# Local attention of one more head pair moved from TensorE to VectorE and GpSimd, and the pace of the later pairs changed

## The chip, the core and the metric

The kernel runs on one core of one Trainium2 chip. The metric is the device time of one execution in microseconds (us), and the time before is the median of three runs. The core's engines run side by side and meet only at semaphores: PE (TensorE, matrix products), DVE (VectorE), ACT (ScalarE), POOL (GpSimd), and the DMA transfers, most of which here are issued from the SP queue. Each engine takes its instructions strictly in the order in which they stand in its own queue.

## The reference

Three stages follow each other. The attention stage has 4 batches of 8 heads, 576 tokens and 64 features per head. Its output is the sum of a pooled attention (over means of 4 neighbouring tokens, repeated 4 times) and a local attention in which a token sees only the 7 tokens at a distance below 4:

```python
factor = 4
q_d = q.reshape(B, H, Sd, factor, D).mean(axis=3)          # k_d, v_d likewise
out_up = np.repeat(sm_attn(q_d, k_d, v_d), factor, axis=2)
mask = np.abs(pos[:, None] - pos[None, :]) < factor
scores = np.where(mask, scale * np.matmul(q, k.transpose(0, 1, 3, 2)), -1e9)
out_local = np.matmul(softmax(scores), v)
x = (out_up + out_local)            # as [2304 tokens, 512]
h = x @ w_in                        # [2304, 2048]
x = (h * sigmoid(1.702 * h)) @ w_out
x = ((x @ w1) * (x @ w2)) @ w3 @ w_out2
```

## The kernel before

**Staging.** The heads are worked in 16 pairs, numbered n = 0 to 15, four to a batch, so pairs 8 to 11 are the third batch and 12 to 15 the fourth. The 2304 tokens of the second stage are cut into five blocks j = 0 to 4 (512, 512, 512, 256 and 512 tokens). Block j is computed while the attention of batch j + 1 is worked in its gaps: block 1 carries pairs 8 to 11, block 2 carries pairs 12 to 15. Block j + 1 begins by reading the attention output `x_d` of its tokens from DRAM (`tok_load`, `tok_split`), and the fourth quarter of the features comes from the last pair of a batch. So block 2 cannot start before pair 11 has been written, nor block 3 before pair 15.

**A block.** For each of 16 slices f of the inner dimension, `h_step` does 12 products of 128x512 into `ps_h` (three passes by `mm3`, since every float32 operand is split into a high and a low part), ACT applies the activation and makes the high part `gh`, DVE the low part `gl` (`split`, L113 and L114). `y_step` for that slice comes two slices later and does 12 more products into `ps_y`. Between these products `pump` puts one piece of the attention at every second place.

**Two ways to do local attention.** The usual way uses TensorE: `s_local` multiplies 64 queries by 72 keys (18 small products per pair, L327), DVE masks and takes the maximum (L330, L331), ACT does the exponentials, `p_piece` transposes nine tiles (L389) and `v_local` does 18 more small products (L416). PSUM tiles of all these steps share the two buffers of pool `pst`: a later step must wait until DVE or ACT has read the tile two steps earlier. For a pair in the table `LOCAL` the work is done without TensorE: `l_load` fetches query, key and value rows (`ql`, `kl`, `vl`), `l_scores` forms a product for each of seven distances o (L457, DVE or for two of them POOL) and sums it (L459, DVE), `l_soft` is the softmax on small tiles (L464 to L471), `l_values` multiplies (L478) and adds (L481), and the result goes to DRAM as `o_d` (L484). `l_out` reads it back transposed (`ost`, L494, L498), adds the pooled part `od` (L501) and writes `x_d` (L504). The pooled attention of every pair stays as it is: `s_pool` (L346, L348), `v_pool` (L404, L407), and for the last batch L371 on DVE.

**Order.** `local_pieces` strings the pairs of `LOCAL` together, 15 pieces a pair after its load. `tick` counts the places between products, from slice 14 of block 0 on, and the number in the table says at every how many places the next piece is put, with a raised priority. The tile framework then schedules the instructions by priority and its own estimates, so the place in the code is not quite the place in an engine's queue. The buffers of pool `stp` (three) hold `ql`, `kl`, `vl`; those of `dp` (two) the products and `ost`.

Of the kernel before, what the change touches and what calls it, by code (L numbers as in the profile page):

```python
# [20 lines left out]
def fused_kernel(ctx, tc, q, k, v, w_in, w_out1, w1, w2, w3, w_out2, out):  # L21
# [20 lines left out]
    PADQ = (NPB - 1) * PB + QB  # L42
    PE_T = 2
    L_F0 = NF - 2
    LOCAL = {12: 3, 13: 3, 14: 4, 15: 4}
    L_PRI = 50
    NM_V = (3,)
    NO = 2 * FAC - 1
# [23 lines left out]
    dram = ctx.enter_context(tc.tile_pool(name="dram", bufs=1, space=DRAM))  # L72
    ldp = ctx.enter_context(tc.tile_pool(name="ldp", bufs=len(LOCAL), space=DRAM))
    psy = ctx.enter_context(tc.tile_pool(name="psy", bufs=1, space=PSUM))
# [157 lines left out]
    def att_load(n, names="qkv", queue=None):  # L232
        b, hp = divmod(n, HP)
        queue = queue or nc.scalar
        for name, src in (("q", q), ("k", k)):
            if name not in names:
                continue
            if b >= PE_T:

                st = att.tile([128, S // 32, 32], F32, tag="s" + name, name="s_" + name)  # L240
                for i in range(4):
                    nc.sync.dma_start(out=st[i * 32:(i + 1) * 32], in_=bass.AP(
                        src.tensor, src.offset + (b * H + 2 * hp + i // 2) * S * D + i % 2 * 32,
                        [[D, 32], [32 * D, S // 32], [1, 32]]))
                at["s" + name, n] = st
                continue
            st = att.tile([UC, 2, FAC, 2, D], F32, tag="s" + name, name="s_" + name)
            for c in range(2):
                queue.dma_start(out=st[:, c], in_=head_ap(
                    src, b, hp, c * UC * FAC, [[FAC * D, UC], [D, FAC], [S * D, 2], [1, D]]))  # L250
            at["s" + name, n] = st
        if "v" not in names:
            return
        st = att.tile([UC, 2, 2, FAC * D], F32, tag="sv", name="s_v")
        queue.dma_start(out=st, in_=head_ap(
            v, b, hp, 0, [[FAC * D, UC], [S * D, 2], [UC * FAC * D, 2], [1, FAC * D]]))
        at["sv", n] = st

    def att_load_v(n):
        b, hp = divmod(n, HP)  # L260
        for t, i0, i1 in ((0, 0, HQ), (1, HQ, NQB)):
            vw = at["vw", n, t] = att.tile([KW, i1 - i0, 2, D], F32, tag=f"vw{t}", name="vw")
            for j0, j1 in ((i0, i0 + 1 - t), (i0 + 1 - t, i1 - t), (i1 - t, i1)):
                tok = min(max(j0 * QB - FAC, 0), S - KW)
                if j1 - j0 == 1:
                    nc.sync.dma_start(
                        out=vw[:, j0 - i0], in_=head_ap(v, b, hp, tok, [[D, KW], [S * D, 2], [1, D]]))
                elif j1 > j0:
                    for h in range(2):
                        nc.sync.dma_start(out=vw[:, j0 - i0:j1 - i0, h], in_=head_ap(  # L270
                            v, b, hp, h * S + tok, [[D, KW], [QB * D, j1 - j0], [1, D]]))
# [63 lines left out]
    def s_pool(n, own_exp):  # L335
        if n % HP == 0 and n > 0:
            att_load(n + 1, "qk")
        near = n not in LOCAL
        if not near:
# [37 lines left out]
    def p_piece(n, i0, i1):  # L377
        if i0 % NPH == 0 and i0 // NPH >= (n in LOCAL):
            at["PT", n, i0 // NPH] = att.tile(
                [KW, min(NPH, NPT - i0), 128], F32, tag=f"PT{i0 // NPH}", name="PT")  # L380
        i0 = i0 if n not in LOCAL else max(i0, NQB)
        ps = pst.tile([KW, i1 - i0, 128], F32, tag="t", name="ps_pt")
        for i in range(i0, i1):
            if i < NQB:
                src = at["el", n][:, i]
            else:
                kc, j = divmod(i - NQB, NPB)
                src = at["ep", n][:, j, kc * UC:(kc + 1) * UC]
            nc.tensor.transpose(ps[:, i - i0], src, ident)  # L389
        nc.scalar.activation(at["PT", n, i0 // NPH][:, i0 % NPH:i0 % NPH + i1 - i0], ps, AF.Copy)  # L390
        first = i0 == (0 if n not in LOCAL else NQB)
        if first:
            v_means(n)
            if n % HP < HP - 1 and n + 2 < B * HP:
                att_load(n + 2, "qk")
# [13 lines left out]
    def v_local(n, i0, i1):  # L409
# [14 lines left out]
        nc.sync.dma_start(out=x_d[:, hp, b * S + i0 * QB:b * S + i1 * QB], in_=xo)  # L424
        if i1 == NQB and n + 1 < B * HP and n + 1 not in LOCAL:
            att_load_v(n + 1)
# [553 lines left out]
```

## Time and profile before

| | us |
|---|---|
| median of 3 runs | 885.12 |
| lowest, highest | 882.38, 891.02 |
| the profiled execution | 888.76 |
| its span, first to last instruction | 886.9 |
| PE busy in the span | 843.2 |
| DVE busy | 589.1 |
| ACT busy | 407.7 |
| POOL busy | 115.2 |

The profile is one execution. Busy shares are means over stages with different limits, so the stage that the change touches (about 240 to 475 us after the span's start) is read by itself.

### The profile page before, as it was taken

The page shows a single profiled execution, that of the slowest core. Times are in us where ns is not written, and L with a number is a line of the kernel's source. Part 1 is how long each engine was busy: PE and PEld are TensorE (multiplying, and loading weights), DVE is VectorE, ACT ScalarE, POOL GpSimd, SP SyncE. Part 2 cuts the span into 40 slices and gives each one's busy share as a digit, 9 for nine tenths or more (in the row PEclk, how much of TensorE's full clock was granted, in tenths as well). Part 3 has the DMA queues.
Part 4 walks back from the last instruction along what each step waited for, and adds up shares of the span by engine and source line. Part 5 has one row for each costly group of instructions (what it writes and reads, how often), then busy time and mean ns, then how long its engine had stood idle before and what let it go on. Part 6 is the DMA issues. An engine that isn't in the chain of part 4 may idle for free.

```text
span 886.9 us, 13686 instructions
## 1 busy us (share of the span) xinstructions
PE 843.2 (95%) x5132; PEld 710.4 (80%) x5132; DVE 589.1 (66%) x1069; ACT 407.7 (46%) x862; POOL 115.2 (13%) x105
## 2 busy tenths in 40 slices
PE   5599989989999999999999999999999999999998
PEld 4477767667677777777789988889999999989996
DVE  5996798779997895847767983253546455545451
ACT  4667677567656666355446663242112211222110
POOL 5323211102342322301200000000000000000000
PEclk9789999999999999999999999999999999999999
DMA  8875784556564344533349988103456364636421
GB/s 226 288 193 154 201 266 144 148 165 175 145 168 98 69 119 101 143 84 74 93 123 355 336 322 334 42 1 111 186 221 253 98 235 177 262 120 234 181 84 71
DMA packets 140598, 150.76 MB, mean 170 GB/s; under 512 B 86898, under 2 KB 121460, under 8 KB 136436
## 3 DMA queue, kind: packets, MB, share of 16 engines
q1 hardware_dynamic: 119424, 141.21, 49.5%
q10 hardware_dynamic: 21108, 8.69, 4.4%
q8 instruction: 40, 0.66, 0.3%
q14 instruction: 26, 0.21, 0.1%
HBM read 117.75 MB, written 32.11 MB: 169 GB/s over the span
## 4 chain that ended last, share of the span: by engine, by line
PE 74%; DVE 12%; DMA 6%; issue 3%; ACT 3%; POOL 1%; SPq 0%; ACTq 0%; DVEq 0%; POOLq 0%
PE ps_ab L119 7%; PE ps_ab L117 7%; PE ps_ab L118 7%; PE ps_h L117 6%; PE ps_y L117 5%; PE ps_h L118 5%; PE ps_y L119 5%; PE ps_h L119 5%; PE ps_y L118 5%; PE ps_o L118 4%; PE ps_o L119 4%; PE ps_o L117 4%; DMA st<-in_moe_w_in_dram 2%; DVE dec L178 2%; DMA st<-in_moe_w_out_dram 2%
## 5 line engine op out<-in xcount | busy, mean ns | idle before, releaser
L117 PE MATMUL ps_h<-x_t,w 128*128 128x512 f32 (+1 forms) x320 | 122.7, 385 | 4.5 <-DVE w L114 4.1
L118 PE MATMUL ps_h<-x_t,w 128*128 128x512 f32 (+1 forms) x320 | 119.7, 374 | 2.7 <-DVE x_t L114 2.7
L117 PE MATMUL ps_y<-gh,w 128*128 128x512 f32 (+1 forms) x320 | 122.1, 382 | 0.0
L118 PE MATMUL ps_y<-gl,w 128*128 128x512 f32 (+1 forms) x320 | 118.8, 371 | 2.1 <-DVE gl L114 2.1
L119 PE MATMUL ps_h<-x_t,w 128*128 128x512 f32 (+1 forms) x320 | 119.1, 372 | 0.0
L119 PE MATMUL ps_y<-gh,w 128*128 128x512 f32 (+1 forms) x320 | 119.0, 372 | 0.0
L119 PE MATMUL ps_ab<-b_t,a_in 128*128 128x384 f32 x336 | 112.5, 335 | 0.0
L117 PE MATMUL ps_ab<-b_t,a_in 128*128 128x384 f32 x336 | 112.5, 335 | 0.0
L118 PE MATMUL ps_ab<-b_t,a_in 128*128 128x384 f32 x336 | 112.4, 334 | 0.0
L114 DVE TENSOR_TENSOR gl<-g_t,gh 128x512 fp32r<-128x512 f32 (+1 forms) x80 | 54.1, 679 | 65.3 <-ACT gh L113 64.8
L618 ACT ACTIVATE g_t<-ps_h 128x512 f32<-128x512 f32 (+1 forms) x80 | 44.3, 555 | 93.6 <-PE ps_h L119 93.3
L113 ACT ACTIVATE abh<-ab 128x384 fp32r<-128x384 f32 x24 | 12.6, 526 | 137.5 <-DVE ab L743 137.5
L117 PEld LDWEIGHTS ps_h<-x_t,w 128*128 128x128 f32 x320 | 60.6, 190 | 18.9 <-DVE w L114 5.9
L118 PEld LDWEIGHTS ps_h<-x_t,w 128*128 128x128 f32 x320 | 61.0, 191 | 13.0 <-DVE x_t L114 4.0
L117 PEld LDWEIGHTS ps_y<-gh,w 128*128 128x128 f32 x320 | 60.3, 189 | 11.8 <-issue 2.4
L118 PEld LDWEIGHTS ps_y<-gl,w 128*128 128x128 f32 x320 | 60.4, 189 | 11.3 <-DVE gl L114 2.7
L119 PEld LDWEIGHTS ps_h<-x_t,w 128*128 128x128 f32 x320 | 60.8, 190 | 10.4 <-issue 0.2
L119 PEld LDWEIGHTS ps_y<-gh,w 128*128 128x128 f32 x320 | 60.4, 189 | 10.4
L117 PEld LDWEIGHTS ps_ab<-b_t,a_in 128*128 128x128 f32 x336 | 63.1, 188 | 0.9
L118 PEld LDWEIGHTS ps_ab<-b_t,a_in 128*128 128x128 f32 x336 | 63.1, 188 | 0.9
L119 PEld LDWEIGHTS ps_ab<-b_t,a_in 128*128 128x128 f32 x336 | 63.1, 188 | 0.0
L178 DVE SCALAR_TENSOR_TENSOR dec<-dec,st 128x512 int32<-128x512 int32 x72 | 57.3, 803 | 2.2 <-ACT dec L165 1.2
(146 smaller groups left out, 1628.7 us busy)
## 6 DMA issues: line engine op xcount, KB each, us to landing
a_in<-a_d SPq DMA_DIRECT2D x24, 1792.0 KB
st<-in_moe_w_dram SPq DMA_DIRECT2D x32, 512.0 KB
a_d<-ap SPq DMA_DIRECT2D x8, 1792.0 KB
st<-in_moe_w_out_dram SPq DMA_DIRECT2D x24, 512.0 KB
st<-in_moe_w_in_dram SPq DMA_DIRECT2D x16, 512.0 KB
yr<-y_d SPq DMA_DIRECT2D x12, 384.0 KB
out_dram<-osb SPq DMA_DIRECT2D x17, 256.0 KB
s_v<-in_v_dram ACTq DMA_DIRECT2D x15, 288.0 KB
```

The costliest lines, as they stand in the source:

```text
L113: nc.scalar.activation(hi, raw, AF.Copy)
L114: lo_eng.tensor_tensor(lo, raw, f32(hi), op=ALU.subtract)
L117: nc.tensor.matmul(ps, ll, rh, start=start, stop=False, skip_group_check=more)
L118: nc.tensor.matmul(ps, lh, rl, start=False, stop=False, skip_group_check=more)
L119: nc.tensor.matmul(ps, lh, rh, start=False, stop=stop, skip_group_check=more)
L178: nc.vector.scalar_tensor_tensor(t, t, 3, st[:, :, 0], op0=ALU.logical_shift_left, op1=ALU.bitwise_or)
L618: nc.scalar.activation(g[:, :n], ps[:, :n], AF.Gelu_apprx_sigmoid)
```

## The change

The table gets an entry for pair 11, the last of the third batch, whose local attention is then done by the second way, at every second place; pairs 14 and 15 go from every fourth place to every third. With pair 11 first in the string, the total is 215 places instead of 214.

```diff
-    LOCAL = {12: 3, 13: 3, 14: 4, 15: 4}
+    LOCAL = {11: 2, 12: 3, 13: 3, 14: 3, 15: 3}
```

PE loses 18 L327, 9 L389 and 18 L416. DVE gains 5 L457, 7 L459, 5 L478, 6 L481, seven small softmax steps, two L498 and two L501, and loses two each of L330, L331, L305 and L420. POOL gains two L457 and two L478 and loses one L369. ACT loses nine exponentials (L307) and two copies (L390) and gains one small exponential.

The first place is DVE's queue in block 1, where `s_local` of pair 10 is reached (`el` is its masked score tile, `prod` the products of a pair of the table). Before:

```order
L481 TENSOR_TENSOR ql_3145<-ql_3145,prod_3616 128x576
L114 TENSOR_TENSOR gl_3442<-g_t_3439,gh_3441 128x512
L330 TENSOR_TENSOR el_3472<-ps_s_3477,band_97 128x360
L331 TENSOR_REDUCE mx_3474<-el_3472 128x5
L305 TENSOR_SCALAR nb_3476<-mx_3474 128x5
L330 TENSOR_TENSOR el_3472<-ps_s_3506,band_97 128x288
L279 STREAM_TRANSPOSE qT_3633<-s_q_3406 128x576
L331 TENSOR_REDUCE mx_3474<-el_3472 128x4
L279 STREAM_TRANSPOSE kT_3658<-s_k_3411 128x576
L305 TENSOR_SCALAR nb_3476<-mx_3474 128x4
L348 TENSOR_REDUCE mx_3474<-ps_sp_3534 128x3
L457 TENSOR_TENSOR prod_3649<-ql_3638,kl_3640 128x576
```

The same place in DVE's queue now:

```order
L481 TENSOR_TENSOR ql_3025<-ql_3025,prod_3448 128x576
L114 TENSOR_TENSOR gl_3459<-g_t_3456,gh_3458 128x512
L457 TENSOR_TENSOR prod_3490<-ql_3480,kl_3482 128x576
L457 TENSOR_TENSOR prod_3543<-ql_3480,kl_3482 128x576
L459 TENSOR_REDUCE s_3489<-prod_3490 128x9
L459 TENSOR_REDUCE s_3489<-prod_3543 128x9
L330 TENSOR_TENSOR el_3496<-ps_s_3501,band_97 128x360
L457 TENSOR_TENSOR prod_3577<-ql_3480,kl_3482 128x576
L331 TENSOR_REDUCE mx_3498<-el_3496 128x5
L459 TENSOR_REDUCE s_3489<-prod_3577 128x9
L305 TENSOR_SCALAR nb_3500<-mx_3498 128x5
L330 TENSOR_TENSOR el_3496<-ps_s_3527,band_97 128x288
```

The first two products and sums of the next pair of the table (pair 13 now, pair 14 before) moved ahead of both L330.

The second place is SP's queue where one pair of the table ends and the next is loaded, first in block 1. Before, the result is written and then the next pair's three tiles are fetched:

```order
L242 DMA s_k_3023<-in_k_dram 32x18x32 x4
L484 DMA o_d_3128<-ql_2662 128x576
L432 DMA ql_3145<-in_q_dram 128x576
L439 DMA kl_3147<-in_k_dram 128x960
L439 DMA vl_3149<-in_v_dram 128x960
```

The same place in SP's queue now:

```order
L432 DMA ql_3025<-in_q_dram 128x576
L242 DMA s_q_3042<-in_q_dram 32x18x32
L637 DMA y_d_93<-ys_2875 128x512
L637 DMA y_d_93<-ys_2881 128x512
L242 DMA s_q_3042<-in_q_dram 32x18x32
L242 DMA s_k_3047<-in_k_dram 32x18x32 x2
L439 DMA kl_3027<-in_k_dram 128x960
L484 DMA o_d_2999<-ql_2662 128x576
```

The fetch of `kl` moved ahead of the write of `o_d`, and that of `ql` further ahead still; the next such place, before pair 13, has `kl` ahead of `o_d` too.

The third place is DVE's queue at the end of block 2, where `l_out` of pair 15 stands (`x_t` is the split input of block 3, `gl` of the last slices of block 2). Before:

```order
L114 TENSOR_TENSOR gl_4849<-g_t_4846,gh_4848 128x512
L498 STREAM_TRANSPOSE xo_4820<-ost_4815 128x320
L501 TENSOR_TENSOR xo_4820<-xo_4820,od_4807 128x320
L178 SCALAR_TENSOR_TENSOR dec_5042<-dec_5042,st_5017 128x512
L498 STREAM_TRANSPOSE xo_4836<-ost_4831 128x256
L501 TENSOR_TENSOR xo_4836<-xo_4836,od_4807 128x256
L114 TENSOR_TENSOR gl_4880<-g_t_4877,gh_4879 128x512
```

The same place in DVE's queue now:

```order
L114 TENSOR_TENSOR gl_4902<-g_t_4899,gh_4901 128x512
L114 TENSOR_TENSOR x_t_4952<-xr_4948,x_t_4952 128x256
L114 TENSOR_TENSOR x_t_4957<-xr_4950,x_t_4957 128x256
L498 STREAM_TRANSPOSE xo_4811<-ost_4806 128x320
L501 TENSOR_TENSOR xo_4811<-xo_4811,od_4798 128x320
L178 SCALAR_TENSOR_TENSOR dec_5033<-dec_5033,st_5008 128x512
L114 TENSOR_TENSOR gl_4933<-g_t_4930,gh_4932 128x512
L498 STREAM_TRANSPOSE xo_4827<-ost_4822 128x256
L501 TENSOR_TENSOR xo_4827<-xo_4827,od_4798 128x256
```

The four steps of `l_out` of pair 15 moved behind the first two `x_t` and to both sides of the last `gl` of the block; before, they stood ahead of the last two `gl` and of every `x_t` of block 3.

## Rows read from the trace of the kernel before

**Rows 1.** The page, part 1: busy us, share of the span, instructions

```profile
PE 843.2 (95%) x5132; PEld 710.4 (80%) x5132; DVE 589.1 (66%) x1069; ACT 407.7 (46%) x862; POOL 115.2 (13%) x105
```

**Rows 2.** Busy us by stretch: length, PE, PEld, DVE, ACT, POOL, clock, DMA, GB/s

```profile
300.00:380.00 80.00, 78.53 (x536) 60.69 (x536) 62.57 (x102) 45.41 (x104) 27.89 (x20) 1.00 0.49 125
...
412.00:460.00 48.00, 48.00 (x247) 37.87 (x246) 31.78 (x60) 21.36 (x43) 5.82 (x5) 1.00 0.44 112
```

**Rows 3.** Timeline, PE, block 1: s_local of pair 11 (start, length)

```profile
339.82 0.40 PE L119 MATMUL ps_h<-x_t,w 128*128 128x512 f32 x1
340.15 0.85 PE L327 MATMUL ps_s<-kT,qT 64*64 64x72 f32 x20
...
341.26 0.39 PE L118 MATMUL ps_y<-gl,w 128*128 128x512 f32 x1
...
342.19 0.40 PE L119 MATMUL ps_y<-gh,w 128*128 128x512 f32 x1
...
343.50 0.40 PE L118 MATMUL ps_y<-gl,w 128*128 128x512 f32 x1
```

**Rows 4.** Timeline, PE: products around a transposing piece, pair 11, then a later pair

```profile
356.38 0.39 PE L119 MATMUL ps_h<-x_t,w 128*128 128x512 f32 x1
...
357.28 0.40 PE L118 MATMUL ps_y<-gl,w 128*128 128x512 f32 x1
...
409.88 0.39 PE L119 MATMUL ps_h<-x_t,w 128*128 128x512 f32 x1
...
410.67 0.39 PE L118 MATMUL ps_y<-gl,w 128*128 128x512 f32 x1
```

**Rows 5.** Timeline, PE: the products around v_local of pair 11

```profile
367.19 0.39 PE L119 MATMUL ps_y<-gh,w 128*128 128x512 f32 x1
...
369.05 0.40 PE L118 MATMUL ps_y<-gl,w 128*128 128x512 f32 x1
```

**Rows 6.** Groups of DVE instructions, 240 to 460 us, shapes apart: busy, mean ns

```profile
L459 DVE TENSOR_REDUCE s<-prod 128x9 f32<-128x576 f32 x28 | 20.3, 744 | 6.2 <-POOL prod L457 6.2
L457 DVE TENSOR_TENSOR prod<-ql,kl 128x576 f32<-128x576 f32 x20 | 18.2, 918 | 4.7 <-DMA kl<-in_k_dram 3.9 <-issue 0.7
```

**Rows 7.** Timeline, PE: its two longest waits from 240 to 480 us

```profile
291.96 0.95 PE L346 MATMUL ps_sp<-kd,qd 64*64 64x144 f32 x12 [1.54 <-DVE el L330]
...
379.86 0.50 PE L118 MATMUL ps_h<-x_t,w 128*128 128x512 f32 x1 [1.30 <-DVE x_t L114]
```

**Rows 8.** Timeline, DVE and SP queue: one pair of the table ends, the next begins

```profile
312.35 1.42 DVE L478 TENSOR_TENSOR prod<-vl,s 128x576 f32<-128x576 f32 x2
...
315.75 0.53 DVE L330 TENSOR_TENSOR el<-ps_s,band 128x360 f32<-128x360 f32 x1
...
321.11 0.76 DVE L457 TENSOR_TENSOR prod<-ql,kl 128x576 f32<-128x576 f32 x1 [0.87 <-DMA kl<-in_k_dram]
...
316.17 0.41 SPq L439 DMA_DIRECT2D kl<-in_k_dram  x1
```

**Rows 9.** Timeline, PE: s_pool of pair 10

```profile
318.63 0.95 PE L346 MATMUL ps_sp<-kd,qd 64*64 64x144 f32 x12
```

**Rows 10.** Timeline, DVE: the same change of pairs, one pair earlier

```profile
278.65 0.76 DVE L457 TENSOR_TENSOR prod<-ql,kl 128x576 f32<-128x576 f32 x1 [3.00 <-DMA kl<-in_k_dram]
```

**Rows 11.** Timeline, DVE: s_pool of pair 15, its maximum and its scaling

```profile
435.54 0.59 DVE L348 TENSOR_REDUCE mx<-ps_sp 128x3 f32<-128x432 f32 x1
...
438.56 0.61 DVE L371 TENSOR_TENSOR ep<-ep,sm 128x432 f32<-128x432 f32 x1
```

**Rows 12.** Timeline, SP queue and DVE: pair 11 written, last input of block 2

```profile
371.26 0.35 SPq L424 DMA_DIRECT2D x_d<-xo  x1
...
379.13 0.68 DVE L114 TENSOR_TENSOR x_t<-xr,x_t 128x512 fp32r<-128x512 f32 x1
```

**Rows 13.** Timeline, DVE and PE: last gl of block 2, first product of block 3

```profile
468.22 0.69 DVE L114 TENSOR_TENSOR gl<-g_t,gh 128x512 fp32r<-128x512 f32 x1
...
474.24 0.28 PE L117 MATMUL ps_h<-x_t,w 128*128 128x256 f32 x1
```

## The prediction

> **What bounds the kernel now.** I read the page first: PE is busy for 843.2 of 886.9 us and DVE for 589.1 [rows 1], so PE sets the pace over the span, and what the change is worth is what it does to PE's stream. Then I cut the span by stages. In 300 to 380 us, the main part of block 1, PE is busy for 78.53 of 80 us and DVE for 62.57 [rows 2]; PE has no slack there and DVE has 17.4 us, but in pieces between waits. Third, PE's timeline from 240 to 480 us, looking for brackets, that is, idle time and who ended it. Two of them are over 1 us [rows 7]: 1.54 us before the `s_pool` of pair 9, whose PSUM buffer DVE had not yet read, and 1.30 us at the start of block 2, where the last quarter of its input arrives late. The rest of this stage runs almost without a gap on PE, so each us of PE work removed here is a us of span, as long as the DVE work that replaces it is never waited for.
>
> **What the change removes from PE.** Products of 128x512 start every 0.23 us when nothing lies between them: the four steps from 341.26 to 342.19 take 0.93 [rows 3]. The cost of an inserted piece is the distance of the products around it less that pitch.
> - `s_local` of pair 11: 339.82 to 341.26 is 1.44 us for two steps, so 0.98 extra, and 342.19 to 343.50 is 1.31, so 0.85 extra [rows 3]. Together 1.83.
> - transposes: a piece of four tiles costs 357.28 - 356.38 = 0.90, less 0.46, so 0.44; a piece of a table pair with three tiles costs 410.67 - 409.88 = 0.79, so 0.33 [rows 4]. Pair 11 has three pieces of four and one of three now and two of three afterwards: 1.65 - 0.66 = 0.99.
> - `v_local`: 369.05 - 367.19 = 1.86, less 0.46, so 1.40 [rows 5].
>
> The sum is 4.2 us, and all of it lies on the path. The nine exponentials and two copies that leave ACT are worth nothing by themselves beyond that, since ACT is busy for 45.41 of these 80 us [rows 2] and ends neither of the two waits [rows 7].
>
> **What it adds to DVE, and where.** 23 of the added instructions pass over 576 elements, at 0.744 (L459) to 0.918 us (L457, with its slow ones beside POOL) [rows 6]: 17 to 21 us, and some 4 us of small ones, less about 3 us of L330, L331, L305 and L420. That is 18 to 22 us. DVE's order says where: to the end of block 1 there are three pairs' values before and after, and only two L457, three L459 and pair 11's `l_out` more, so block 1 takes about 3 us net and block 2 the other 16 or so. Added up, DVE can hold it. What counts is the order in the queue, at four places.
>
> *First change of pairs.* Pair 12's `kl` is now fetched ahead of the write of pair 11's result. Before, DVE sat idle for 3.00 us for that fetch and began the next scores at 278.65 [rows 10]; those scores stand ahead of the `el` step whose lateness cost PE 1.54 us [rows 7]. If they start 2 to 3 us earlier, that wait shrinks to little. I take 1.3 us of gain, between a gain of 1.5 and, should the two transposes that now stand among the scores eat it up, a loss of 1.
>
> *Second change of pairs, the new wait.* This is the step I trust least and the largest cost. At pair 10's `s_local`, two L457 and two L459 of pair 13 now stand ahead of the L330 that frees the PSUM buffer for `s_pool`. L457 must wait for `kl`. By the rows of the same place: the last L478, which frees the buffer for `kl`, ends at 313.77; before, `kl` was issued at 316.17 and used at 321.11, 4.94 us later, with `ql` and the result's write in flight beside it [rows 8]. Issued at 313.8, it would be usable at 318.7. Four instructions take 2.8 and L330 0.53 (it ran at 315.75 before, at no one's expense [rows 8]), so the buffer is free at 322.1. PE wanted it at 318.5, since L346 began at 318.63 [rows 9]. PE then waits 3.6 us, with everything behind L346 in its queue. Bounds: if the fetch takes half as long, being issued first now, 1.1; if `kl` in the end goes out no sooner than before, 4.94 from 316.17 and then 3.3, that is 324.4, so 5.9; and none if DVE runs further ahead of PE here than it did. I take 3.6.
>
> The Trainium skill, page "DMA: Bandwidth & Descriptors", section "Anatomy of one DMA — SWDGE (gpsimd) path", fits a transfer as about 2.0 us fixed plus its bytes at 436 GB/s, for transfers that GpSimd issues. An estimate by it is 3.1 us for these 480 KB, the wait would be 1.8 us and the whole sum 1.8 us lower; the row above, with its companions in flight, is longer and no run of this kernel shows the fetch alone.
>
> *Start of block 2.* Pair 11's last step on PE is now `v_pool`, 24 products (5.5 us) earlier in PE's queue than `v_local` was with respect to block 2, which covers DVE's two L498 and two L501 and the write. The last input step came at 379.13, 7.9 us after the write was issued at 371.26 [rows 12]; moved ahead by that much, it stands clear of the need. So the wait of 1.30 us [rows 7] goes: a gain of 1.3, or none if `l_out` is itself held up by pair 14's scores, among which its steps are placed.
>
> *Pair 15's `s_pool`.* Before, DVE took 435.54 to 439.17 from L348 to the end of L371, with 6 instructions between [rows 11]. Now 21 stand between: seven long ones more (0.744 to 0.918 [rows 6], 5.8 us), four `l_out` steps (estimate 0.45 each, from the 0.53 of L330 [rows 8]) and four small ones (0.2 each, an estimate), so 8.4 us longer, 12.0 in all, counted from the end of L346, 0.95 after its start: 13.0. PE has in the meantime L346 (0.95), `v_pool` (0.7, an estimate by the same row) and 45 products of 0.23, so 12.0. It waits 1.0 us; bounds 0 and 3, since waits for POOL's products can come on top.
>
> *Start of block 3.* Pair 15's `l_out` now stands behind the first two `x_t` and around the last `gl`, which cannot run before the last `h_step`; it began at 468.22, and block 3 at 474.24 [rows 13]. The second L501 then ends at about 469.8. Block 3 needs its fourth quarter after nine products of half width, at 475.3: 5.5 us for the write, the read and two splits, which took 8.6 at the start of block 2 with twice the width and other transfers beside it [rows 12]. I take a wait of 1.0, between 0 and 3.1. Before, there was none.
>
> **Sum.** -4.2 - 1.3 - 1.3 + 3.6 + 1.0 + 1.0 = -1.2 us. The profiled execution took 888.76 us, 1.9 more than its span and 3.6 more than the median, 885.12. So 887.6 for an execution like it, and 883.9 as a median.
>
> **Rivals.**
> - *The cover holds.* `kl` lands before DVE gets to it, and none of the new waits appears. For it: DVE has 17.4 us idle in 300 to 380 [rows 2], and the fetch is issued earlier. Against it: four instructions in front of L330 are a matter of the order and not of the load. Then -4.2 - 1.3 - 1.3 = -6.8, so 878.3.
> - *Pair 15 is late and block 3 waits (slower).* Its scores now start behind pair 14's L348, so that about 12 us of DVE work moved into the last 50 us of block 2, and then `o_d` must be written, read back, added, written as `x_d` and read again. Without the last term the sum is -2.2, so from a wait of 2.2 us on at block 3 the change loses. For it: the chain of 8.6 us [rows 12] against the 5.5 us left, and `l_out` placed as late as it can be. Against it: the stretch needs only about 44 of 48 us of DVE (31.78 before [rows 2] and the 12), and the transfer is half as wide. With a wait of 6 us the time is 885.1 - 2.2 + 6 = 888.9; to lose 1% it would have to be 11.
> - *The change does not do what it says.* PE's queue has lost exactly the three groups of pair 11, so this has almost no chance.
>
> **How the numbers follow.** The forecast, gains and new waits that nearly cancel (881 to 887), gets 0.60; the cover that holds, 0.20; the late pair 15, 0.17; anything else 0.03. The range of 8 in 10 reaches to both rivals: 877.5 to 890. A change under 1%, 8.9 us, can hardly be told from none. Faster by over that needs every gain and something unseen: 0.05. Slower by over that needs the late pair at its worst together with the 5.9 us: 0.06. Within it 0.89.
>
> **What would show it.** In the profile of the changed kernel: PE's busy time down by some 4 us; an idle bracket of 2 to 5 us before L346 ended by DVE `el` at pair 10, about 315 us in, with L457 waiting for `kl` just ahead of it; no bracket of over 0.5 us at that place for pair 9 nor at the first `x_t` of block 2; brackets of about 1 us before pair 15's L389 and in the first slice of block 3. I am wrong if PE is idle elsewhere in blocks 1 and 2, above all before a `ps_y` product that waits for `gl`, for then DVE's total, and not its order, has become the bound.

## The result, and the profile after

The changed kernel took 894.43 us (median of 9 runs, 889.16 to 899.68) beside 885.12 us before: ratio 1.0107, 95% interval 1.0083 to 1.0132. It is slower by 1.1%. The forecast was 883.9 with a range up to 890.0, so it was wrong, in its sign and in its range.

The page's part 1, in the profiled execution (894.43 us, span 892.6), answers to [rows 1]:

```profile
PE 842.0 (94%) x5051; PEld 708.7 (79%) x5051; DVE 609.7 (68%) x1095; ACT 407.1 (46%) x847; POOL 119.0 (13%) x108
```

The work moved as forecast: 81 PE records fewer (each of the 36 small products of L327 and L416 is recorded twice, each of the nine transposes once), and 20.6 us more on DVE, where 18 to 22 were expected. But PE is busy for almost as long as before, where 4.2 us less were expected, and it waits more. The windows of the changed kernel (length, PE, PEld, DVE, ACT, POOL, clock, DMA, GB/s) show where; the first and the last answer to [rows 2], and the two in between cover the longest new waits:

```profile
300.00:380.00 80.00, 74.93 (x450) 57.91 (x449) 66.76 (x105) 39.01 (x80) 24.65 (x19) 0.98 0.44 109
345.00:353.00 8.00, 5.21 (x46) 3.77 (x46) 6.46 (x14) 3.94 (x9) 1.56 (x2) 0.79 0.72 222
380.00:391.00 11.00, 8.39 (x37) 5.66 (x36) 10.74 (x14) 4.30 (x8) 2.98 (x2) 0.84 0.38 84
412.00:460.00 48.00, 46.34 (x241) 36.58 (x240) 36.78 (x64) 22.03 (x41) 8.96 (x7) 1.00 0.29 66
```

In those two short windows the kernel before has PE busy for all 8.00 and 11.00 us, at a granted clock of 1.00. Now PE stands, and the mean granted clock falls to 0.79 and 0.84 besides. PE's timeline from 240 to 480 us gives the brackets (idle time and who ended it) of over 0.5 us (answers to [rows 7]):

```profile
278.75 0.63 PE L389 MATMUL ps_pt<-ident,el 128*72 128x128 f32 x4 [1.35 <-POOL el L369]
...
319.31 0.71 PE L404 MATMUL ps_vp<-PT,vd 72*64 72x144 f32 x8 [0.51 <-DVE el L330]
...
328.42 1.27 PE L416 MATMUL ps_v<-PT,vw 72*64 72x64 f32 x36 [1.37 <-ACT ep L307]
...
348.46 0.80 PE L416 MATMUL ps_v<-PT,vw 72*64 72x64 f32 x20 [2.79 <-ACT ep L307]
...
386.60 0.52 PE L118 MATMUL ps_y<-gl,w 128*128 128x512 f32 x1 [2.36 <-DVE gl L114]
...
455.08 0.82 PE L389 MATMUL ps_pt<-ident,ep 128*72 128x128 f32 x6 [1.66 <-DVE ep L371]
```

Both waits of before are gone (1.54 at `ps_sp`, 1.30 at `x_t`), and six others are there, 10.0 us in all. The last was in the forecast as it came, and the second is a small remnant of another forecast wait (see the part on the second change of pairs below); the other four, 7.9 us, were not.

The longest one, followed back. PE has `v_local` of pair 10 in its queue and needs a PSUM buffer; the buffer holds `ps_sp` of pair 11 until ACT has taken its exponentials, and these wait for the maximum (L348) and its scaling (L305) on DVE, which stand behind pair 13's values:

```profile
342.00 1.41 DVE L478 TENSOR_TENSOR prod<-vl,s 128x576 f32<-128x576 f32 x2
343.33 1.28 DVE L481 TENSOR_TENSOR ql<-ql,prod 128x576 f32<-128x576 f32 x1
344.54 0.59 DVE L348 TENSOR_REDUCE mx<-ps_sp 128x3 f32<-128x432 f32 x1
345.06 0.68 DVE L114 TENSOR_TENSOR gl<-g_t,gh 128x512 fp32r<-128x512 f32 x1
345.66 0.15 DVE L305 TENSOR_SCALAR nb<-mx 128x3 f32<-128x3 f32 x1
...
345.91 1.28 ACT L307 ACT_TABLE_LOAD   x1 [4.76 <-DVE nb L305]
...
347.94 0.38 ACT L307 ACTIVATE ep<-ps_sp,nb 128x144 f32<-128x144 f32 x1
...
351.40 0.63 PE L118 MATMUL ps_h<-x_t,w 128*128 128x512 f32 x1
351.83 0.63 PE L119 MATMUL ps_h<-x_t,w 128*128 128x512 f32 x1
```

The last two rows show the second price: after that wait products start every 0.43 us instead of 0.23, the lower of PE's two levels. ACT adds to the first: of the 2.5 us from its start at 345.91 until the buffer is read, 1.28 are the load of its table for the exponential.

The wait of 1.37 us at 328.42, for the exponentials of `s_pool` of pair 10, has another chain. Its scaling ended on DVE at 322.73, but ACT came to those exponentials only at 325.36. ACT had stood until 318.97 for the scaling of pair 10's local scores, which had pair 13's scores ahead of it on DVE, and then loaded its table three times, as a step of the activation (L618) stood between the local exponentials and the pooled ones:

```profile
322.03 0.70 DVE L305 TENSOR_SCALAR nb<-mx 128x3 f32<-128x3 f32 x1
...
318.97 1.28 ACT L307 ACT_TABLE_LOAD   x1 [8.14 <-DVE nb L305]
...
323.44 1.28 ACT L618 ACT_TABLE_LOAD   x1
...
325.36 1.28 ACT L307 ACT_TABLE_LOAD   x1
```

The wait at 386.60 is the one that the prediction named as the sign of its own failure. The `gl` of the first slice of block 2 stands behind pair 14's values:

```profile
383.57 0.75 DVE L478 TENSOR_TENSOR prod<-vl,s 128x576 f32<-128x576 f32 x1
384.35 1.59 DVE L481 TENSOR_TENSOR ql<-ql,prod 128x576 f32<-128x576 f32 x1
385.86 0.68 DVE L114 TENSOR_TENSOR gl<-g_t,gh 128x512 fp32r<-128x512 f32 x1
```

The big products of the second stage are the same 1920 in every kernel here (128x512, those of block 3 128x256), so their starts serve as milestones. The table gives the time from one of them to the next in us, worked out from the traces (block 1 starts at number 384, block 2 at 768, block 3 at 1152):

| kernel | 384 to 480 | to 576 | to 660 | to 768 | to 830 | to 1010 | to 1152 | sum |
|---|---|---|---|---|---|---|---|---|
| before | 27.4 | 32.3 | 26.1 | 33.4 | 17.2 | 48.9 | 33.8 | 219.2 |
| changed | 27.7 | 30.5 | 28.3 | 33.5 | 20.9 | 48.7 | 35.6 | 225.1 |
| pace alone | 26.7 | 31.4 | 26.1 | 33.4 | 21.2 | 49.2 | 33.5 | 221.5 |
| pair alone | 28.4 | 37.3 | 27.4 | 30.9 | 15.7 | 48.6 | 35.7 | 224.1 |
| without pair 11's local attention | 32.8 | 30.5 | 27.7 | 29.7 | 20.2 | 48.7 | 36.1 | 225.7 |
| pause | 29.5 | 30.5 | 28.2 | 34.7 | 15.2 | 48.6 | 36.1 | 222.9 |
| no maximum | 28.5 | 30.5 | 27.3 | 29.2 | 19.3 | 48.7 | 33.9 | 217.4 |
| pause, no maximum | 29.8 | 30.6 | 27.3 | 29.2 | 16.6 | 48.7 | 34.4 | 216.5 |
| before, no maximum | 26.7 | 31.6 | 26.1 | 33.4 | 15.6 | 49.2 | 33.5 | 216.2 |
| those two, norm first | 28.1 | 30.5 | 27.3 | 29.2 | 16.6 | 48.7 | 34.4 | 214.7 |

A sum is one execution, and single ones differ by some us. That of before was 3.6 us above its median, and part of this lies in the table: the pace alone, and the pace with the pause (further down), have the same order as before in the queues of PE, DVE, ACT and GpSimd from number 384 to 576, and take 58.1 and 58.5 us for it instead of 59.7. The wait of 1.54 us at `ps_sp` is 0.61 and 0.63 there:

```profile
285.97 0.95 PE L346 MATMUL ps_sp<-kd,qd 64*64 64x144 f32 x12 [0.61 <-DVE el L330]
...
293.33 0.95 PE L347 MATMUL ps_sp<-kd,qd 64*64 64x144 f32 x12 [0.63 <-DVE el L331]
```

So the loss of 5.9 us in the table is less than the 9.3 between the medians, and no trace shows all of the difference. Verdicts below go by the runs; the table says only where.

### The profile page after: what moved, and what is told of

It reads as the page before. It is cut to its first block, busy times and chain, and to the rows that moved or that the text cites. A ratio compares the mean times of both kernels' runs of the same rounds, so it can differ in the third digit from the quotient of the medians.

```text
span 892.6 us, 13551 instructions
## 1 busy us (share of the span) xinstructions
PE 842.0 (94%) x5051; PEld 708.7 (79%) x5051; DVE 609.7 (68%) x1095; ACT 407.1 (46%) x847; POOL 119.0 (13%) x108
## 4 chain that ended last, share of the span: by engine, by line
PE 70%; DVE 15%; DMA 6%; issue 4%; ACT 3%; POOL 1%; ACTq 0%; SPq 0%; DVEq 0%; POOLq 0%
PE ps_ab L117 7%; PE ps_ab L119 7%; PE ps_ab L118 7%; PE ps_h L117 5%; PE ps_y L117 5%; PE ps_y L119 5%; PE ps_y L118 5%; PE ps_h L118 5%; PE ps_h L119 5%; PE ps_o L118 4%; PE ps_o L119 4%; PE ps_o L117 4%; DVE dec L178 3%; DMA st<-in_moe_w_out_dram 2%; DVE ql L481 2%
## 5 line engine op out<-in xcount | busy, mean ns | idle before, releaser
L114 DVE TENSOR_TENSOR gl<-g_t,gh 128x512 fp32r<-128x512 f32 (+1 forms) x80 | 51.7, 648 | 58.8 <-ACT gh L113 58.5
L618 ACT ACTIVATE g_t<-ps_h 128x512 f32<-128x512 f32 (+1 forms) x80 | 44.1, 553 | 85.6 <-PE ps_h L119 81.0
```

What stands on the lines that cost most here:

```text
L114: lo_eng.tensor_tensor(lo, raw, f32(hi), op=ALU.subtract)
L618: nc.scalar.activation(g[:, :n], ps[:, :n], AF.Gelu_apprx_sigmoid)
```

## The experiments

Theory A: pair 11's DVE work comes ahead of short steps that PE needs soon. Rival B: the pace of pairs 14 and 15 does it. Rival C: DVE's total has become the bound. Ratios are to runs of the kernel before on the same chip, with the 95% interval.

### The change taken apart

```diff
-    LOCAL = {11: 2, 12: 3, 13: 3, 14: 3, 15: 3}
+    LOCAL = {12: 3, 13: 3, 14: 3, 15: 3}           # pace alone
+    LOCAL = {11: 1, 12: 2, 13: 3, 14: 4, 15: 4}    # pair alone
```

> Only the new pace: pairs 14 and 15 at every third place, pair 11 stays on PE as before. Theory A (pair 11's added DVE work, put into DVE's in-order queue in blocks 1 and early 2, stands ahead of short steps that PE needs soon): the waits of ps_v for ACT's exponentials and of ps_y for gl go, the start of block 2 keeps its 1.30 us wait, and the time is 885 (883 to 888). Rival B (it is the faster pace of pairs 14 and 15 that crowds DVE in block 2): the waits stay in good part and the time is 890 to 895. Rival C (DVE's total work is the bound): the work is that of the kernel before, so 885, but then the waits should also be spread over many places in the changed kernel.

> Only the pair: pair 11's local attention on DVE and GpSimd, pairs 14 and 15 keep every fourth place; to fit, pair 11 goes at every place and pair 12 at every second. Theory A (pair 11's work ahead of short steps): PE still waits for several us in blocks 1 and 2, 889 to 895. Rival B (the pace of 14 and 15): the waits go, PE's saving of 4.2 us shows, 881 to 885. Rival C (DVE's total): as the changed kernel, 894.

The pace alone: 888.70 us, 1.0058 (1.0028 to 1.0089). The pair alone: 891.76, 1.0103 (1.0076 to 1.0129). So neither A nor B alone: each part loses. In the table the pace loses at one place, the start of block 2 (21.2 against 17.2). The pair alone passes that place in 15.7, and loses in block 1, 37.3 against 32.3 before number 576, where its trace has two waits of 2.90 and 3.27 us for GpSimd's `el`.

```diff
+                if n == 11:                        # local_pieces; x_d of pair 11 then gets od alone
+                    yield lambda: None, 1 + 15 * every
+                    continue
```

> The changed kernel without pair 11's local attention: neither PE nor DVE and GpSimd compute it (its places stay empty, and its x_d holds the pooled part alone). All theories have PE's saving here; what remains is the saving without its price on DVE. Saving as predicted: 885.1 - 4.2 - 1.3 - 1.3 = 878 to 881, and no wait of over 1 us for DVE or ACT in blocks 1 and 2. If the loss is from the pace of pairs 14 and 15 (rival B), waits remain in block 2 and the time is 886 to 890.

> Pair 11's local attention is done twice: on PE as before the change, and its DVE and GpSimd steps run too, in the places of the changed kernel, with a result that nobody uses. So PE has none of the saving and DVE has all of the added work. If the cost of the added DVE work is separate from the saving: 894.4 + 4.2 = 898.6 (896 to 902). If PE's own work covers DVE's (the longer PE takes, the later it needs DVE): close to the changed kernel, 892 to 895.

Without any local attention of pair 11: 891.94, 1.0092 (1.0062 to 1.0122), a miss for all three theories. From 660 to 768 PE takes 29.7 instead of 33.4, so the saving is there; but the waits for `gl` (3.08 us) and for pair 15's L371 (1.89) stay though DVE has none of pair 11's work, and an input wait of 3.07 us comes at the start of block 1. What is late in block 2 is late though DVE has no more to do than before (busy for 591.0 us in all, 589.1 before); what has changed is where the pairs behind pair 11 stand. This speaks against C. With the work done both ways: 895.40, 1.0138 (1.0111 to 1.0165), 0.3% over the changed kernel, where 0.5% was the saving by itself; the intervals overlap, so this decides nothing.

### Steps put ahead by priority

```diff
+            with tc.high_priority(100):      # scores first: all steps of s_local, s_pool from pair 8 on
+        with tc.high_priority(100 if j > 0 else 0):   # split first: gelu, gh, gl
-    L_PRI = 50
+    L_PRI = 0                                # no priority
```

> The changed kernel, with the scores of the pairs of the later batches (L330, L348, the maxima and L305) put ahead of the local pieces in DVE's queue. Theory A (order in DVE's queue): the two waits of ps_v for the exponentials (4.2 us, and the low clock behind them) go or shrink under 1 us, so 5 to 6 us come back: 888 to 890; the waits for gl at 386 us and for pair 15's L371 stay. Rival C (DVE's total, or what the tables of places do to the whole stretch): the waits come back elsewhere, 893 to 896.

> The changed kernel, with the gelu and the split into gh and gl of all slices but the first of a batch put ahead of the local pieces. Theory A: the wait of 2.4 us for gl in block 2's first slice goes, with the low clock behind it, 3.5 us in all: 890 to 892; the two waits of ps_v stay. Rival C: no change, 893 to 896.

> Both orders together. Theory A: about 9 us of the loss come back and PE's saving shows, 884 to 887. Rival C: 892 to 896. A second rival: local pieces pushed back make the later pairs late (pair 15's L371 and l_out), then a longer wait at 455 us or a new one at the start of block 3, 888 to 892.

> The changed kernel with the local pieces given no priority at all (L_PRI 0 in place of 50), so that each stands in DVE's queue where the program writes it. Theory A: if their early place is what makes PE wait, the waits of ps_v and of gl shrink: 886 to 890; if the written places already stand ahead of the short steps, no change, 893 to 896. Rival C: 893 to 896.

Scores first 894.03 (1.0109, 1.0089 to 1.0130), split first 894.21 (1.0109, 1.0081 to 1.0138), both 909.48 (1.0277, 1.0246 to 1.0307), no priority 898.38 (1.0159, 1.0136 to 1.0182). None gained. These edits were too broad to decide between A and C: a priority on a piece moves its products too, and PE's queue differs from the changed kernel's in some 20 (no priority) to 50 places (both). With both first, PE's timeline has the scores scattered singly among the products:

```profile
277.01 0.34 PE L327 MATMUL ps_s<-kT,qT 64*64 64x72 f32 x2
277.28 0.50 PE L117 MATMUL ps_y<-gh,w 128*128 128x512 f32 x1
277.71 0.34 PE L327 MATMUL ps_s<-kT,qT 64*64 64x72 f32 x2
```

From 277.28 to the next product at 277.97 is 0.69 us instead of 0.23, and eighteen products in a row take 0.69 to 0.82; four waits of 1.2 to 2.3 us for the input, the activation and GpSimd's `el` stand in front (7.0 us). So PE needs 44.7 us from 384 to 480. Narrower edits came next.

### One wait at a time

The first edit keeps the local pieces off the start of block 2 and catches up afterwards; PE's queue keeps its order but for pair 15's last steps. The second takes DVE out of the chain in front of `ps_v`: the pooled scores of pairs 8 to 15 go to the exponential without their maximum.

```diff
-                if wait[0] <= 0:
+                place[0] += 1
+                if wait[0] <= 0 and not 136 <= place[0] < 152:
                     fn, wait[0] = next(local, (None, 1))
+                    wait[0] = wait[0] if place[0] < 152 else 2
```

```diff
-        nc.vector.tensor_reduce(mx, ps, op=ALU.max, axis=X)
-        if own_exp:
+        flat = own_exp and n >= 2 * HP
+        if not flat:
+            nc.vector.tensor_reduce(mx, ps, op=ALU.max, axis=X)
+        if flat:
+            for i in range(NPB):
+                nc.scalar.activation(ep[:, i], ps[:, i], AF.Exp, scale=PSCALE, accum_out=sm[:, i:i + 1])
+        elif own_exp:
```

> The changed kernel, with no local piece put from place 136 to 152 (the last slice of block 1 and the first of block 2), and one at every second place after that. PE's queue stays as it is but for pair 15's transposes. Theory D (PE waits where DVE's queue is full over some 10 us, whatever its total): the wait of 2.4 us for gl at the start of block 2 and the low clock behind it go (3.7 us), so 889 to 891, and 888 if pair 15's wait of 1.7 us goes too, since its pieces end 10 places earlier; the two waits of ps_v in block 1 stay. Rival C (DVE's total): the waits come back in block 2, where DVE now has as much to do in less time, 893 to 897.

> The changed kernel, where the pooled scores of pairs 8 to 15 go to the exponential without the maximum taken off first, so that ACT no longer waits for L348 and L305 on DVE. Order theory: the two waits of ps_v for ACT's exponentials (4.2 us, and about 1 us at the low clock behind them) go, 888 to 890; the wait for gl at the start of block 2 stays. If ps_v then waits for something else in the same place, 893 to 895.

> Both: the pause at the start of block 2 and the pooled scores without their maximum. If the two losses are separate, both gains add: 894.4 - 5 - 5 = 884 (882 to 887), at or under the kernel before, and PE's saving of 4 us shows in block 1. If DVE's total is the bound, 891 to 895.

> The kernel before, with the pooled scores of pairs 8 to 15 without their maximum: a control for the other two. Its trace shows only 0.5 us of wait for ACT's exponentials, so the edit should give it at most that and some DVE time: 883 to 886. If it gains as much as the changed kernel does (4 us or more), then it was not pair 11's move that made these steps late.

The pause: 891.12, 1.0080 (1.0056 to 1.0104). No maximum: 888.75, 1.0056 (1.0034 to 1.0079). Both: 883.82, 0.9987 (0.9969 to 1.0005). The kernel before without the maximum: 884.54, 1.0007 (0.9986 to 1.0029). Each edit takes away its own wait: with the pause nothing over 0.4 us is left at the start of block 2 (15.2 against 20.9), while the two of `ps_v` stay at 1.37 and 2.78; without the maximum these are 0.94 and none, while `gl` stays at 2.35. Together they give back the whole loss, 1.2% of the time, and the control shows that the second is worth nothing to the kernel before: it was the move of pair 11 that made these steps late. Alone they give 0.3%, which the intervals do not set apart from none, and 0.5%. That both give more than the sum is within the intervals of the four ratios (0.2% each way), and in the table the gains are 2.2, 7.7 and 8.6 us, so not more than the sum.

The second edit does more than it was meant to. The two `ps_v` stand four and five products earlier in PE's queue, with less cover than in the changed kernel. But `s_pool` of pair 15 moves as well, from number 1007 to 999 (972 before), and the wait of 1.66 us for its L371 is gone (33.9 against 35.6 in the last column). And ACT loads its table 25 times from number 384 to 1152, as in the kernel before, where the changed kernel has 29. So not all that this edit gives back need come from the maximum, and these runs don't separate the three. Nor was the pause given to the kernel before, whose trace has a wait of 1.30 us at that place. What PE still waits for with both, from 260 to 480 us:

```profile
277.98 0.63 PE L395 MATMUL ps_pt<-ident,el 128*72 128x128 f32 x4 [2.04 <-POOL el L375]
...
326.24 1.27 PE L422 MATMUL ps_v<-PT,vw 72*64 72x64 f32 x36 [0.94 <-ACT ep L354]
...
378.16 0.50 PE L119 MATMUL ps_y<-gl,w 128*128 128x512 f32 x1 [0.59 <-DVE gl L115]
```

### Where the saving stays

With both edits PE's 4.2 us are visible (29.2 against 33.4 to number 768), and yet the kernel only equals the one before. The wait at 277.98 is at the first change of pairs, where the prediction booked a gain: pair 12's scores now start earlier, and stand ahead of the two small steps (L365, L366) after which GpSimd scales pair 8's `el`. In the changed kernel:

```profile
275.12 1.02 DVE L365 TENSOR_SCALAR sm<-sm 128x12 f32<-128x12 f32 x1
...
276.81 0.22 DVE L366 RECIPROCAL sm<-sm 128x12 f32<-128x12 f32 x1
...
274.68 1.43 POOL L457 TENSOR_TENSOR prod<-ql,kl 128x576 f32<-128x576 f32 x1 [12.08 <-DVE s L459]
277.18 1.52 POOL L369 TENSOR_TENSOR el<-el,sm 128x648 f32<-128x648 f32 x1 [1.07 <-ACT g_t L618]
```

```diff
+        with tc.high_priority(60 if n // HP == 2 else 0):    # norm first: L365, L366 and the scalings
```

> As the kernel with both edits (pause, pooled scores without maximum), and the normalisation of pairs 8 to 11 (L365, L366 of the kernels before) put ahead of the local pieces; in DVE's queue only pair 8's two steps move, ahead of one L457 and two L459, and PE's queue keeps its order but for two products. Order theory: PE's wait of 2.04 us at 278 us for GpSimd's el of pair 8 goes, because the sums reach GpSimd about 2 us earlier: 883.8 - 2 = 882 (881 to 883). If GpSimd's own queue is what is late there (its L457 ahead of the scaling), no change, 883 to 885.

> As the kernel with both edits, and the local scores of pairs 8 to 15 without their maximum too: 22 instructions less on DVE, some 8 us over blocks 1 and 2. If DVE's load in those blocks still costs PE about 5 us (the saving of 4 us is in, the kernel stands at 883.8), part of it comes back: 879 to 882. If only single places in the order matter, 882 to 886, as they fall.

> The kernel before with pooled and local scores of pairs 8 to 15 without maximum: the control for the run with 22 instructions less. 40 instructions less on DVE than before. Since its PE waits for DVE only at two places (1.5 and 1.3 us), it gains at most 3 us: 882 to 885. If it gains as much as the changed kernel, pair 11's move is worth nothing once DVE is eased.

Norm first: 882.18, 0.9976 (0.9951 to 1.0001); the wait shrinks from 2.04 to 0.50, and 384 to 480 from 29.8 to 28.1. No maximum in the local scores either (22 DVE instructions less): 885.77, 1.0025 (0.9995 to 1.0055), no gain over 883.82, and its control 883.25, 0.9988 (0.9955 to 1.0020). So less work on DVE buys nothing that can be measured. Two small steps moved ahead of three long ones buy 1.7 us in that stretch of the traces; by the runs it is 0.1%, with intervals that overlap, so the gain in time is not shown. The run without pair 11's work, the pace alone (DVE busy for 590.1 us, and a loss) and the run with 22 instructions less all speak against C.

### The pace by itself

> The faster pace of pairs 14 and 15 alone (pair 11 on PE as before), with no local piece from place 136 to 152, around the start of block 2. The pace alone took 888.7, with 3.9 us lost at the start of block 2. Theory D: that loss goes, 884 to 886. If the pace costs wherever it is, 888 to 890.

The pace with the pause: 889.49, 1.0067 (1.0038 to 1.0097), as without it. So the local pieces at the start of block 2 are not what the pace alone pays for. The timeline of the pace alone, without the pause, PE and DVE:

```profile
370.38 0.49 PE L117 MATMUL ps_h<-x_t,w 128*128 128x512 f32 x1
373.57 0.79 PE L118 MATMUL ps_h<-x_t,w 128*128 128x512 f32 x1 [2.71 <-DVE x_t L114]
374.17 0.63 PE L119 MATMUL ps_h<-x_t,w 128*128 128x512 f32 x1
374.59 0.63 PE L117 MATMUL ps_h<-x_t,w 128*128 128x512 f32 x1
...
371.51 1.41 DVE L459 TENSOR_REDUCE s<-prod 128x9 f32<-128x576 f32 x2 [1.31 <-POOL prod L457]
372.84 0.68 DVE L114 TENSOR_TENSOR x_t<-xr,x_t 128x512 fp32r<-128x512 f32 x1
```

The last input step starts 4.5 us after the block's first product (368.34), in the kernel before after 4.8 (379.13 [rows 12] less 374.32). But before, six products of the block's second slice stand in PE's queue ahead of those that need it (the wait is at number 784, here at 778): 1.4 us less cover. And behind the longer wait 13 products run at 0.43 instead of 0.23, which is 2.6 us. The two make the 4.0 that the table shows.

```diff
+            with tc.high_priority(100 if kk == KD - 1 and j in (2,) else 0):   # (1, 2) in the second kernel
                 tok_split(j, kk)
```

> The faster pace of pairs 14 and 15 alone, with the split of the last quarter of block 2's input put ahead of the local pieces; with that edit PE's queue has products of the second slice ahead of those that need this quarter (in the pace alone they stand behind). The pace alone lost 3.9 us at the start of block 2, in a wait of 2.71 us for that quarter and 13 products at the low clock behind it. If that wait is the whole price of the pace: 888.7 - 4 = 884.7 (883 to 886). If the pace costs DVE's place elsewhere in block 2: 887 to 889.

> The kernel with three edits (pause, pooled scores without maximum, normalisation of pairs 8 to 11 first), with the last quarter of the input of blocks 1 and 2 split first as well. Its PE still waits 0.70 us for that quarter at the start of block 1 and 0.62 us for gl in block 2: 881 to 882.2; if moving these steps makes others late, 882.5 to 885.

With that input split first the pace alone takes 886.65, 1.0034 (1.0015 to 1.0053): the wait is 1.69 and no product runs slowly behind it. If this is the gain that the ratios show (0.6% to 0.3%, with intervals that overlap), it explains somewhat under half of the pace's loss; the rest stays open. The changed kernel with the three edits and this one takes 880.72, 0.9976 (0.9954 to 0.9997), 0.2% under the kernel before and 1.3% under the changed one.

## Why the prediction was wrong, point by point

- **What PE saves, 4.2 us.** Right: 33.4 to 29.2 where nothing else is late. In the changed kernel itself the waits of `ps_v` hide it.
- **First change of pairs, a gain of 1.3.** Right in its direction, too large: the wait of 1.54 is gone, and 480 to 576 takes 1.8 less than in the trace of before. But with the order of before that wait was 0.6 us in two other executions, so about half of the gain belonged to the one that was profiled. And the same earlier scores made pair 8's `el` late, 1.35 us, which was not looked for; moved back, those two steps gave 1.7 us in the trace.
- **Second change of pairs, a new wait of 3.6.** Mis-sized: at L346 it did not come. Three steps of the order were as said (the fetch, two L457 and two L459, L330), but all of it ran earlier:

```profile
309.27 0.35 SPq L439 DMA_DIRECT2D kl<-in_k_dram  x1
...
312.80 1.43 DVE L457 TENSOR_TENSOR prod<-ql,kl 128x576 f32<-128x576 f32 x2 [1.53 <-DMA kl<-in_k_dram]
...
315.47 0.52 DVE L330 TENSOR_TENSOR el<-ps_s,band 128x360 f32<-128x360 f32 x1
...
316.25 0.95 PE L346 MATMUL ps_sp<-kd,qd 64*64 64x144 f32 x12
```

  `kl` went out at 309.27, not at the 313.8 that was taken from the trace of before [rows 8], and was used 3.5 us later, not 4.9. What was left of the wait came at the next step that needs a buffer of the pair, `v_pool`: 0.51 us for the second L330 of pair 10, which still had pair 13's scores ahead of it. The estimate of 3.1 us from the Trainium skill, page "DMA: Bandwidth & Descriptors", section "Anatomy of one DMA — SWDGE (gpsimd) path", lies nearer to the trace than mine, although it is for transfers that GpSimd issues.
- **Start of block 2, a gain of 1.3.** The input is in time (a wait of 0.22 instead of 1.30, [rows 7]). But PE then stands for 2.36 us before `ps_y`, and the stretch lengthens by 3.7. The prediction had said that such a wait would mean that DVE's total is the bound. The sign was right and its reading wrong: the pause took it away with the same DVE instructions (1095).
- **Pair 15, 1.0.** Right in kind, 1.66 in size. DVE took 12.5 us from L348 (442.40) to the end of L371 (454.93), where 12.0 were added up [rows 11]:

```profile
442.40 0.61 DVE L348 TENSOR_REDUCE mx<-ps_sp 128x3 f32<-128x432 f32 x1 [1.40 <-PE ps_sp L346]
...
454.32 0.61 DVE L371 TENSOR_TENSOR ep<-ep,sm 128x432 f32<-128x432 f32 x1
```

- **Start of block 3, 1.0.** No wait. The slower rival was right in its sign and wrong in its mechanism.

**The step that failed** is "What counts is the order in the queue, at four places". It is order that counts, but the places were those at which a table pair begins or ends. The loss is at steps of other pairs that I never held against the new order: `s_pool` of pairs 10 and 11, whose exponentials stand between PE and a PSUM buffer and came late behind pair 13's steps on DVE (1.37 and 2.79 us), the first `gl` of block 2 (2.36), and the normalisation of pair 8 (1.35). The check that would have found them is, for every short DVE step that frees something for PE, what stands ahead of it now; I made it for L330 of pairs 9 and 10 and L371 of pair 15 only. And no term of the sum had PE's clock in it, though the two longest waits of the changed kernel, 2.36 and 2.79 us, were each followed by products at the lower level.

## What to carry to other kernels

Work put on an engine that "has room" was paid for here by the short steps behind it in its queue: list those that free a buffer or feed the busiest engine, and see for each what now stands ahead. When a scheduler sets the order, one entry of a table can move every later pair, so look at all of the stretch and not at the seams. And cure one wait with an edit that leaves the busiest engine's queue alone, and look at what else it moved; broad priorities moved that engine's work too, and cost up to 1.7% more.

## What the runs showed of the hardware

- **A wait can cost more than its length.** After the waits of 2.36 and 2.79 us in the changed kernel, and of 2.71 in the pace alone, the granted clock fell to the lower level (1.2 GHz) and products took 0.43 us, for 3 to 13 of them. Length alone does not decide it: after the waits of 1.30 and 1.54 before [rows 7], 1.69 with the input first and 2.04 with both edits none ran slowly, but none either after 2.35 without the maximum and after 2.90 and 3.27 in the pair alone, where the granted clock stayed at 1.00; and after one of 1.99 at 236.66 in the changed kernel some did (mean clock 0.80 from 232 to 240 us).
- **A tiny DVE step held up by GpSimd.** L365 on 12 elements a partition took 1.02 us in the changed kernel and ended at 276.14, as GpSimd's L457 (274.68 and 1.43 long) ended at 276.11; with norm first, where it ran just ahead of that product, it took 0.17:

```profile
274.33 0.17 DVE L372 TENSOR_SCALAR sm<-sm 128x12 f32<-128x12 f32 x1
...
274.55 1.90 POOL L464 TENSOR_TENSOR prod<-ql,kl 128x576 f32<-128x576 f32 x1 [10.89 <-DVE sm L372]
```

  The Trainium skill, page "SBUF — State Buffer", section "SBUF: two separate sides", says that GpSimd shares a pair of ports with DVE instructions that run in a 2-port mode or have two inputs from SBUF, and that whichever of the two starts first holds the pair for the whole instruction while the other blocks. These rows agree with it if L365 ran in such a mode, which no row shows. Two scalings of the changed kernel look the same: L305 on 4 and 3 elements, at 320.71 and 322.03, took 0.74 and 0.70 us and ended within 0.03 us of GpSimd's steps at 319.99 and 321.38. By these rows a moved GpSimd product can delay a small DVE step as much as a long DVE one does.
